# Three products moved between engines and one copy split: a linear-attention and MLP-mixer kernel

## The chip, the cores and the metric

The kernel runs on one core of a Trainium2 chip. The metric is the device time of one execution in microseconds (us), as the median of several runs. A core has five engines with a queue each: TensorE (PE) multiplies matrices and transposes, VectorE (DVE), ScalarE (ACT) and GpSimd (POOL) work element by element, SyncE (SP) issues loads and stores. An engine works off its queue in the order of the program and waits where an operand of the next instruction isn't there yet. TensorE writes its results to PSUM; VectorE and ScalarE read them there; GpSimd works on SBUF.

## The reference

```python
# token mixing: r, k, v of shape (4, 8, 768, 48), per batch and head
state = 0
for t in range(768):
    cur = (u * k[t]) outer v[t]
    y[t] = r[t] @ (state + cur)
    state = w * state + k[t] outer v[t]
# x: (4, 768, 384), heads side by side; then an MLP mixer
h  = relu(x^T @ w_tok1) @ w_tok2         # over the tokens, 768 -> 256 -> 768
u_ = x + h^T
h2 = relu(u_ @ w_ch1) @ w_ch2            # over the channels, 384 -> 1536 -> 384
out = u_ + h2
```

## The kernel before

The 768 tokens of a batch are cut into 6 chunks of 128; the 4 batches give 24 units, numbered 0 to 23, six to a batch. Units 0 to 5 are batch 0 and make the start of the kernel. The steps of a unit, by the names of the code:

- kp and rp: the products of k and of r with a decay table (wn, wp), on GpSimd or VectorE, written to the two halves of a tile kpr. The tables are made on ScalarE from the logarithm of w.
- trk and trr: four transposes each on TensorE, of the k half and of the r half. Both write to one tile tr_ps, which lies in one PSUM bank.
- rkk and rkr: two copies of tr_ps into SBUF (tile rk) on ScalarE. For the units in `rk_two` (0, 1, 2, 3, 4, 6) they are two steps, and each can stand in the queue where its own transposes are done. For the others one step rk issues both copies behind trr.
- at: eight matmuls that give the scores of the 8 heads, in two PSUM tiles (even and odd heads). AT0 and AT1: the two halves multiplied by a triangular mask and written to SBUF in bf16, on VectorE. For the units in `raw` (0, 1, 5, 8, 11) the second half goes another way: raw copies it from PSUM to SBUF on ScalarE, and ATr on VectorE multiplies that copy by a bf16 mask.
- pr, pg, yd: the term of the current token (product, small matmul, product with v).
- kv and S: the state, accumulated in PSUM, and its masked copy; every third copy uses a decay table wGm, a product that is made once, behind gd on ScalarE.
- yS and y: matmuls of r with the state and of the scores with v, into one PSUM tile. x adds yd and writes the unit's output as bf16, on VectorE.
- hid and what follows are the mixer: hid multiplies each x by the first token weight and accumulates over the six units of the batch.

The order on each engine is written by a planner (class `Plan`, function `graph`): it simulates the steps with assumed durations, ranks and due times, and gives each step an engine and a start; the steps are then emitted in the order of their starts. Into gaps of TensorE's plan it puts idle matmuls (`fill`). So the order on an engine is fixed when the program is built, and a step that waits holds up all that stands behind it on its engine.

`products_in_turn` adds waits: a product on GpSimd that stands near a product on VectorE is put behind a VectorE instruction, so that the two don't run side by side. Here rp2 is put behind pr0 and rp3 behind AT1 of unit 1, because kp2 and wGm are planned on VectorE.

In queue order, as far as it is touched: GpSimd has kp0, rp0, kp1, rp1, rp2, kp3, rp3, kp4, the issue of the first token weight, rp4, the issue of the second, kp5, rp5, and the issues of five channel weights. ScalarE has rkk3, rkr3, S3, rkk4, vb4 (a cast of v), rkr4, S4, rk5 (two copies), vb5, raw5. TensorE has at4, trk5, pg4, trr5, yS4, a fill, y4, at5. SyncE issues the loads of units 0 to 5 at once; those of unit 6 and on are held until y5.

All instructions go through one helper, so the profile gives nearly all of them one line; they are told apart by tile and shape (kpr<-ld_k is kp, kpr<-ld_r is rp, rk<-tr_ps the copies, at_ps<-rk the scores, AT the masked halves).

Of the kernel before, what the change touches and what calls it, by code (L numbers as in the profile page):

```python
# [45 lines left out]
class Plan:  # L46
# [83 lines left out]
    def fill(self, since, until, least, margin, each, emit):  # L130

        mine = sorted((s for s in self.steps if s.engine == "PE"), key=lambda s: s.start)
        for a, b in zip(mine, mine[1:]):
            if b.start > until:
                break
            if a.end < since:
                continue
            taken = sum(1 for x in self.used if x[0] < b.start and x[1] > a.end)
            n = int((b.start - a.end - margin) / each)
            if b.start - a.end >= least and taken < self.banks and n > 0:  # L140
                s = self.add(f"fill{a.name}", [("PE", n * each, n * each)], emit=emit(n))
                s.engine, s.start, s.end, s.seen = "PE", a.end, a.end + n * each, a.end + n * each
        return sorted(self.steps, key=lambda s: s.start)


def products_in_turn(steps, apart):


    both = [s for s in steps if s.engine in ("DVE", "POOL") and s.name.rstrip("0123456789") in ("kp", "rp", "ku", "rku", "yd", "wGm")]
    dve = [s for s in steps if s.engine == "DVE"]  # L150
    behind, d = {}, None
    for s in both:
        if s.engine == "DVE":
            d = s if len(s.after) and s.name[:2] != "yd" or s.ways[0][0] == "POOL" else d
        elif d is not None and s.start - d.end < apart:
            n = dve.index(d)
            behind[s] = dve[n - 1] if n and d.start - dve[n - 1].end < 0.05 else d
            d = None
    return behind
# [9 lines left out]
def graph(do, cfg):  # L169
# [246 lines left out]
CFG = dict(apart=2.0,   # L416
    transfers=[("u", u) for u in range(0, 6)]
    + [('k', 6)]
    + [('r', 6)]
    + [('k', 7)]  # L420
    + [('r', 7)]
    + [('v', 6)]
    + [('v', 7)]
    + [('u', 8)]
# [20 lines left out]
    xload={6: 0.33},  # L445
    wtime=(3.0, 2.6, 1.55, 5.2, 3.1, 3.9, 1.55),
    raw=(0, 1, 5, 8, 11),
    rk_two=(0, 1, 2, 3, 4, 6),
    mix=(0.0, 0.0, -1.0, -2.6),
    off3=[{}, {}, {'AT0': -0.12, 'rp': 0.83, 'rku': 1.35}],  # L450
# [17 lines left out]
def kernel(  # L468
# [121 lines left out]
    for i in range(NB):  # L590
        t = const.tile([128, 2, H, P], bf16, name=f"kpr{i}")
# [24 lines left out]
    wGm = const.tile([128, HP, 2, D], f32, name="wGm")  # L616
# [387 lines left out]
    def do(kind, *args):  # L1004
        return lambda eng: STEPS[kind](eng, *args)

    def fill(eng, n):
        t = psM.tile([128, 512], f32, name="fill_ps", tag="m")
        for lo in range(0, n, 2):
            cols = slice(0, 256 * min(2, n - lo))  # L1010
            pe.matmul(t[:, cols], idle[:, 0:128], idle[:, cols], start=True, stop=True)

    plan = graph(do, CFG)
    steps = plan.run()
    if CFG.get("fill"):
        first = next(s for s in steps if s.name == "z0_0_0").start
        steps = plan.fill(CFG.get("fill_from", 0.0), first, *CFG["fill"], lambda n: lambda eng: fill(eng, n))
    behind = products_in_turn(steps, CFG["apart"])
    last = {}
    for s in steps:  # L1020
# [38 lines left out]
```

## Time and profile before

| | |
|---|---|
| median of 3 runs | 165.36 us (164.93 to 165.66) |
| profiled execution | 165.7 us, of it span 164.0 us |
| TensorE busy | 156.6 us |
| VectorE busy | 109.2 us |
| ScalarE busy | 88.5 us |
| GpSimd busy | 67.1 us |

The span runs from the first to the last instruction of the profiled execution; the other 1.7 us of its time lie around it. A row of the timeline gives the start in us, the duration, the engine, the operation with its output and inputs, the number of instructions that are merged in it and, in brackets, how long the engine sat idle before it and what ended that. A row of the chain of waits gives start, duration and the work that the end of the kernel was waiting for at that time.

### The profile page before, as it was taken

Reading aid. Unit: us, or ns where it says so; the run is one execution under the profiler, and the core shown is the slowest. Engines: PE = TensorE matmul, PEld = TensorE weight load, DVE = VectorE, ACT = ScalarE, POOL = GpSimd, SP = SyncE. Lnnn points to the kernel's source line nnn. Section 1 sums busy time; section 2 is a strip of 40 time slices with the busy share of each in tenths; the row PEclk is TensorE's granted clock in tenths of the full one; section 3 lists DMA queues with packets and bytes.
Section 4 is the critical chain, followed back from the end, with each engine's and each line's share of the span. In section 5 each row is a group of like instructions: output and inputs, shape, how many; then the busy total and the mean of one; then the engine's idle time right before and its main releaser. Section 6 shows DMA issues by size and latency. Waiting matters only on the chain.

```text
span 164.0 us, 3852 instructions
## 1 busy us (share of the span) xinstructions
PE 156.6 (95%) x1466; PEld 100.9 (62%) x1466; DVE 109.2 (67%) x225; ACT 88.5 (54%) x194; POOL 67.1 (41%) x83
## 2 busy tenths in 40 slices
PE   6798999999999999899999999999999999999992
PEld 3277865566677666566566565666656655666562
DVE  6679897602289889899899899977876582012021
ACT  3898662595488466789706450077253502914900
POOL 8748893000037848566875856204750000000000
DMA  4999999999798997999999972999990028012012
GB/s 92 221 223 207 173 154 173 192 194 232 153 231 233 190 213 220 196 238 180 217 231 133 263 135 67 203 231 194 194 240 4 0 53 216 19 52 96 0 48 96
DMA packets 87307, 26.26 MB, mean 160 GB/s; under 512 B 76665, under 2 KB 87290, under 8 KB 87290
## 3 DMA queue, kind: packets, MB, share of 16 engines
q1 hardware_dynamic: 83392, 22.88, 65.1%
q0 software_dynamic: 3888, 3.15, 13.1%
q8 instruction: 11, 0.18, 0.4%
q14 instruction: 6, 0.05, 0.2%
q10 hardware_dynamic: 10, 0.00, 0.0%
HBM read 20.65 MB, written 4.72 MB: 155 GB/s over the span
## 4 chain that ended last, share of the span: by engine, by line
PE 85%; DVE 5%; ACT 5%; issue 2%; POOL 1%; DVEq 0%; ACTq 0%
PE h_ps L515 33%; PE z_ps L515 29%; PE y_ps L515 5%; PE at_ps L515 5%; PE tr_ps L515 4%; PE hT_ps L515 3%; PE kv_ps L515 3%; ACT rk L515 2%; DVE AT L515 2%; DVE x_b L515 1%; PE w_ps L515 1%; DVE yd L515 1%; POOL kpr L515 1%; ACT wp L515 1%; ACT raw L515 1%
## 5 line engine op out<-in xcount | busy, mean ns | idle before, releaser
L515 ACT ACTIVATE zr<-z_ps 128x384 bf16<-128x384 f32 x94 | 45.4, 492 | 44.2 <-PE z_ps L515 44.1
L515 PE MATMUL z_ps<-uT,wch 128*128 128x384 bf16 x288 | 52.5, 326 | 0.2
L515 PE MATMUL h_ps<-wch,zr 128*128 128x384 bf16 (+1 forms) x300 | 52.5, 320 | 0.0
L515 PEld LDWEIGHTS <-zr 128*128 128x128 bf16 x300 | 27.9, 98 | 15.5 <-issue 0.2
L515 PEld LDWEIGHTS <-wch 128*128 128x128 bf16 x288 | 26.7, 98 | 16.1 <-issue 0.4
L515 POOL TENSOR_TENSOR yd<-vb,adg 128x384 f32<-128x384 bf16 x18 | 15.5, 859 | 42.2 <-ACT adg L515 25.1
L515 DVE TENSOR_TENSOR AT<-at_ps,mask 128x512 bf16<-128x512 f32 x43 | 27.9, 683 | 0.6 <-PE at_ps L515 0.5
L515 DVE TENSOR_TENSOR osb<-u_sb,h_ps 128x384 f32<-128x384 bf16 (+1 forms) x22 | 11.7, 532 | 23.5 <-PE h_ps L515 23.4
L515 POOL TENSOR_TENSOR kpr<-ld_r,wp 128x384 bf16<-128x384 f32 x16 | 17.0, 1064 | 5.3 <-DVE yd L515 2.2
L515 ACT COPY rk<-tr_ps 128x512 bf16<-128x512 bf16 x28 | 15.5, 589 | 5.5 <-PE tr_ps L515 5.1
L515 PEld LDWEIGHTS <-kpr 128*128 128x128 bf16 x192 | 13.6, 108 | 6.1 <-POOL kpr L515 2.6
L515 DVE TENSOR_TENSOR x_b<-y_ps,yd 128x384 bf16<-128x384 f32 x24 | 13.3, 552 | 5.8 <-PE y_ps L515 5.5
L515 POOL TENSOR_TENSOR kpr<-ld_k,wn 128x384 bf16<-128x384 f32 x15 | 15.5, 1031 | 2.1 <-PE z_ps L515 1.1
L515 PEld LDWEIGHTS <-rk 48*128 48x128 bf16 (+1 forms) x272 | 11.1, 100 | 6.4 <-issue 2.8
L515 PE MATMUL tr_ps<-ident,kpr 128*128 128x128 bf16 x112 | 12.3, 247 | 2.0 <-ACT rk L515 1.0
L515 ACT CAST vb<-ld_v 128x384 bf16<-128x384 f32 x24 | 12.3, 511 | 3.5 <-DMA ld_v<-in_v_dram 3.5
L515 DVE TENSOR_TENSOR u_sb<-x_b,hT_ps 128x384 bf16<-128x384 bf16 x21 | 10.4, 546 | 1.1 <-PE hT_ps L515 1.1
L515 PEld LDWEIGHTS <-wtok 128*128 128x128 bf16 x90 | 8.0, 98 | 4.8 <-issue 0.6
L515 PEld LDWEIGHTS <-AT 128*128 128x128 bf16 x192 | 8.6, 99 | 3.6 <-DVE AT L515 0.7
L515 PE MATMUL at_ps<-rk 48*128 48x128 bf16 x192 | 10.4, 233 | 0.4 <-ACT rk L515 0.4
L515 DVE TENSOR_TENSOR kpr<-ld_k,wn 128x384 bf16<-128x384 f32 x9 | 5.9, 658 | 7.0 <-DMA ld_k<-in_k_dram 7.0
L515 PE MATMUL h_ps<-x_b,wtok 128*128 128x384 bf16 x48 | 10.2, 326 | 0.1
(91 smaller groups left out, 154.2 us busy)
## 6 DMA issues: line engine op xcount, KB each, us to landing
ld_k<-in_k_dram SPq DMA_DIRECT2D x24, 192.0 KB, 3.6
ld_v<-in_v_dram SPq DMA_DIRECT2D x24, 192.0 KB, 3.7
out_dram<-osb SPq DMA_DIRECT2D x23, 192.0 KB, 2.5
ld_r<-in_r_dram SPq DMA_DIRECT2D x28, 96.0 KB, 3.2
ld_r<-in_r_dram SPq DMA_DIRECT2D x10, 192.0 KB, 3.8
wch<-in_moe_w_ch_dram POOLq DMA_DIRECT2D x3, 576.0 KB, 12.6
wtok<-in_moe_w_tok_dram POOLq DMA_DIRECT2D x2, 384.0 KB, 5.1
wch<-in_moe_w_ch_dram POOLq DMA_DIRECT2D x2, 288.0 KB, 5.6
```

What stands on the lines that cost most here:

```text
L515: ins = tc.keep_in_program_order(f(*args, **kw))
```

## The change

A new function `placed` edits the finished plan, behind the planner and the fills, so that no other step changes its place.

- kp2 goes from VectorE to GpSimd at the same place in the order (behind rp1). wGm goes from VectorE to GpSimd, just ahead of rp2. With no such product on VectorE, `products_in_turn` no longer puts rp2 and rp3 behind a VectorE instruction.
- For units 2, 3 and 4, a step raw is put on ScalarE behind the unit's at, and the second half of the scores is masked from that copy (ATr) at its old place on VectorE. On ScalarE raw2 stands between rkk3 and rkr3, raw3 between vb4 and rkr4, raw4 behind S4.
- For unit 5, the copy of the k half is a step rkk5 of its own, put on ScalarE behind trk5 (and behind raw4). In the order of the program it now stands ahead of trr5. The old step copies only the r half.

```diff
+def placed(steps, do, moved, raw, apart):
+    named = {s.name: s for s in steps}
+    for u in raw:
+        s = Step(f"raw{u}", [], (), None, (), 0.0, do("raw", u))
+        s.engine, s.start = "ACT", named[f"at{u}"].end + 0.001
+        s.end = s.seen = s.start + 0.6
+        named[f"AT1_{u}"].emit = do("ATr", u)
+        steps.append(s)
+    for u in apart:
+        s = Step(f"rkk{u}", [], (), None, (), 0.0, do("rkk", u))
+        s.engine, s.start = "ACT", named[f"trk{u}"].end + 0.001
+        s.end = s.seen = s.start + 0.5
+        named[f"rk{u}"].emit = do("rkr", u)
+        steps.append(s)
+    for name, engine, other in moved:
+        s, t = named[name], named[other]
+        s.engine = engine
+        if s is not t:
+            s.start = s.end = s.seen = t.start - 1e-6
+    return sorted(steps, key=lambda s: s.start)
...
     raw=(0, 1, 5, 8, 11),
+    raw_too=(2, 3, 4),
+    rk_apart=(5,),
+    moved=(('kp2', 'POOL', 'kp2'), ('wGm', 'POOL', 'rp2')),
...
+    steps = placed(steps, do, CFG["moved"], CFG["raw_too"], CFG["rk_apart"])
     behind = products_in_turn(steps, CFG["apart"])
```

## The prediction

> **What bounds the kernel now.** I read the page first, for the engine that is full.
>
> ```profile
> span 164.0 us, 3852 instructions
> PE 156.6 (95%) x1466; PEld 100.9 (62%) x1466; DVE 109.2 (67%) x225; ACT 88.5 (54%) x194; POOL 67.1 (41%) x83
> ```
>
> TensorE is busy for 156.6 of 164.0 us. The waits of TensorE from 30 us to the end come next:
>
> ```profile
> PE at_ps L515 <- ACT rk L515: 0.4, 1, 0.4
> PE kv_ps L515 <- ACT vb L515: 0.2, 1, 0.2
> ```
>
> Behind 30 us it waits for 0.6 us in all. So whatever the start gains or loses reaches the end nearly whole, and nothing behind it makes up for it. The change lies ahead of 27 us, so I followed the chain of waits there (start, us, what).
>
> ```profile
> 12.78 0.59 ACT raw L515
> ...
> 16.42 0.20 PE g_ps L515 x4
> ...
> 18.89 0.33 PE y_ps L515 x8
> ...
> 19.24 0.56 DVE x_b L515
> ...
> 26.55 0.57 DVE x_b L515
> ...
> 27.16 0.48 PE h_ps L515 x2
> ```
>
> There are three stretches. Up to 13.9 us ScalarE's queue sets the pace, from 13.9 to 19.24 TensorE, from 19.24 to 27.16 VectorE, until x of unit 5 lets the last token-mixing matmuls of batch 0 start at 27.16. The time of that start is what I work out; a shift of it is a shift of the end. The timeline of TensorE shows the joints:
>
> ```profile
> 13.91 0.59 PE L515 MATMUL tr_ps<-ident,kpr 128*128 128x128 bf16 x4 [0.67 <-ACT rk L515]
> ...
> 17.83 0.63 PE L515 MATMUL tr_ps<-ident,kpr 128*128 128x128 bf16 x4
> ...
> 18.25 0.63 PE L515 MATMUL fill_ps<-idle 128*128 128x512 bf16 x1
> ...
> 19.79 0.38 PE L515 MATMUL tr_ps<-ident,kpr 128*128 128x128 bf16 x4
> ...
> 20.89 0.58 PE L515 MATMUL y_ps<-vb,AT 128*128 128x48 bf16 x8
> 21.41 0.40 PE L515 MATMUL at_ps<-rk 48*128 48x128 bf16 x8
> 21.73 0.40 PE L515 MATMUL tr_ps<-ident,kpr 128*128 128x128 bf16 x4
> ...
> 22.14 0.40 PE L515 MATMUL tr_ps<-ident,kpr 128*128 128x128 bf16 x4
> 22.38 0.33 PE L515 MATMUL y_ps<-S,rk 128*128 128x96 bf16 x4
> 22.55 0.81 PE L515 MATMUL fill_ps<-idle 128*128 128x512 bf16 x3
> 23.20 0.19 PE L515 MATMUL y_ps<-vb,AT 128*128 128x48 bf16 x1
> 23.58 0.35 PE L515 MATMUL y_ps<-vb,AT 128*128 128x48 bf16 x7 [0.20 <-DVE AT L515]
> 23.86 0.40 PE L515 MATMUL at_ps<-rk 48*128 48x128 bf16 x8
> ...
> 25.94 0.45 PE L515 MATMUL y_ps<-vb,AT 128*128 128x48 bf16 x8
> 26.23 0.33 PE L515 MATMUL at_ps<-ident,x_b 128*128 128x128 bf16 x3
> ```
>
> By the order of the code: 13.91 is trr2 (transposes of r, unit 2); 17.83 trk4; 19.79 trr4; 20.89 y3; 21.41 at4 (scores of unit 4); 21.73 trk5 and 22.14 trr5; 22.38 yS4; 22.55 the idle fill; 23.20 and 23.58 y4; 23.86 at5; 25.94 y5.
>
> **Parts 1 and 2: k product of unit 2 and decay table to GpSimd.** The rows of both engines:
>
> ```profile
> 10.64 0.55 DVE L515 TENSOR_TENSOR kpr<-ld_k,wn 128x384 bf16<-128x384 f32 x1
> ...
> 14.69 0.55 DVE L515 TENSOR_TENSOR wGm<-bm,wG 128x384 f32<-128x384 f32 x1
> ```
>
> ```profile
> 12.31 1.13 POOL L515 TENSOR_TENSOR kpr<-ld_r,wp 128x384 bf16<-128x384 f32 x1 [2.24 <-DVE yd L515]
> ...
> 14.85 1.25 POOL L515 TENSOR_TENSOR kpr<-ld_r,wp 128x384 bf16<-128x384 f32 x1 [0.46 <-DVE AT L515]
> ...
> 17.00 0.89 POOL L515 DMA_DIRECT2D wtok<-in_moe_w_tok_dram  x1
> 18.37 0.99 POOL L515 TENSOR_TENSOR kpr<-ld_r,wp 128x384 bf16<-128x384 f32 x1 [0.48 <-DMA ld_r<-in_r_dram]
> ...
> 21.08 1.01 POOL L515 TENSOR_TENSOR kpr<-ld_r,wp 128x384 bf16<-128x384 f32 x1
> ```
>
> GpSimd sits idle from 10.07 to 12.31 (2.24). Two products of 0.99 (the row alone) to 1.25 (the row beside the table on VectorE) take 2.0 to 2.5 us there, so rp2 is 0 to 0.3 late, and ends at 13.44 to 13.74. trr2 starts at 13.91 behind a ScalarE copy, so either end is hidden; I take 0.1. Without that cover it would be the 0.3. VectorE is 2 x 0.55 us lighter, and that is worth nothing either: before 13.9 ScalarE's fixed order sets the pace, after it TensorE does.
>
> In the Trainium skill, "GPSIMD Engine Reference", section "Engine selection", sends two-input elementwise work to VectorE, GpSimd being about twice as slow, and the rows here agree on that ratio (0.55 against 0.99). By that rule taken as a cost on the path the two moves would lose 2 x 0.44 us; by the rows they lose nothing, being under the idle time.
>
> One thing does move. rp3 (14.85) is kept in turn behind a VectorE product only because the table stood on VectorE; that wait goes. kp3 ends at 14.39 (14.85 less 0.46), so rp3 starts up to 0.46 earlier and takes 0.99 for 1.25. kp4 and the issue of the first token-mixing weight (17.00) then come up to 0.7 us earlier, among loads of r, k and v that still run: a rival below.
>
> **Part 3: half the scores of units 2, 3, 4 through ScalarE.** The rows that price it, VectorE first:
>
> ```profile
> 19.78 1.29 DVE L515 TENSOR_TENSOR AT<-at_ps,mask 128x512 bf16<-128x512 f32 x2
> ...
> 24.97 0.68 DVE L515 TENSOR_TENSOR AT<-at_ps,mask 128x512 bf16<-128x512 f32 x1
> 25.57 0.42 DVE L515 TENSOR_TENSOR AT<-raw,mask_b 128x512 bf16<-128x512 bf16 x1
> 25.90 0.55 DVE L515 TENSOR_TENSOR yd<-vb,g_ps 128x384 f32<-128x384 bf16 x1
> ```
>
> ```profile
> 13.27 0.59 ACT L515 COPY rk<-tr_ps 128x512 bf16<-128x512 bf16 x1
> ...
> 22.58 1.07 ACT L515 COPY rk<-tr_ps 128x512 bf16<-128x512 bf16 x2 [1.23 <-PE tr_ps L515]
> ...
> 24.33 0.59 ACT L515 CAST raw<-at_ps 128x512 bf16<-128x512 f32 x1 [0.26 <-PE at_ps L515]
> ```
>
> From start to next start VectorE spends 0.60 on a half read from PSUM (24.97 to 25.57) and 0.33 on one read from SBUF: 0.27 saved each, for a 0.59 us copy on ScalarE. Unit 2 lies in TensorE's stretch: nothing. Unit 3: y3 starts at 20.89 behind the fill as before, but no longer waits inside for the second half. Unhindered y5 passes in 0.29 (25.94 to 26.23, the next matmuls' start), so at4 starts at 21.18 instead of 21.41. Unit 4: VectorE ends its halves about 0.54 earlier, so y4's wait (23.20 to 23.58) would be gone. Left alone, this part gains between 0.2 (only at4's shift) and 0.5 us (below).
>
> **Part 4: k of unit 5 copied apart.** This is where I expect the gain to go. The two halves of one tr tile lie in one PSUM bank, and in the new order the copy of the k half stands between trk5 and trr5. Unit 2 has that order already: its k copy on ScalarE runs 13.27 to 13.86, its r product was ready at 13.44, and trr2 starts at 13.91 with "0.67 <-ACT rk". So transposes into the second half wait for the copy of the first. In the old order trr5 (22.14) followed rp5 (ends 22.09) at once.
>
> In the Trainium skill, "PSUM — Partial Sum Buffer", section "PSUM bank collisions raise a hardware error", says that two engines must not touch one bank and quadrant at once, and that software has to order them; unit 2's wait agrees, 0.05 us behind the copy's end. By that rule trr5 waits always; by the one row alone it might not, which is the second rival.
>
> The sum: at4 21.18, ends 21.58 (0.40). raw4 0.07 later (raw5 came 0.07 behind at5's end, 24.26 to 24.33): 21.65. The copy of k5 stands behind it in ScalarE's queue, 0.49 later (12.78 to 13.27): 22.14, ends 22.73. trr5 22.78, which is 0.64 later than now. TensorE issues in order, so yS4, the fill and y4 stand behind it: 0.24 + 0.17 + 0.65 (22.14 to 22.38, 22.55, 23.20) gives y4 23.84, its halves long ready. at5 0.29 later: 24.13, against 23.86. Its r copy: trr5 ends 23.18, copied to 23.81, in time. From at5 to y5 TensorE has 2.08 us of work and no idle time (23.86 to 25.94): y5 26.21, ends 26.66, x5 about 26.70 against 26.55. The start at 27.16 becomes 27.31: **+0.15 us**. So the wait inside y4 is taken away and a longer one at trr5 takes its place.
>
> Bounds of this part: if at4 does not come earlier, everything is 0.23 later, +0.38; if trr5 is not held, -0.5.
>
> The profiled execution took 165.7 us by itself, so it becomes 165.85. The median of the runs is 165.36, 0.34 lower, with runs from 164.93 to 165.66; against the median I forecast **165.5 us**. About 0.5%, 0.8 us, is what a measurement of this kernel can tell from no change.
>
> **Rivals.** *trr5 is not held* (164.9). Then trr5 stays at 22.14, y4 runs whole at 23.20, at5 starts at 23.49, 0.37 earlier; y5 25.57 to 26.02; x5 at 26.06, 0.49 earlier than now. Against it: the 0.67 at trr2.
>
> *The early weight issue delays r of unit 4* (165.8). rp4 waits for its load until 18.37 (0.48). If the weight's 0.7 us earlier start costs that load 0.65, rp4 ends at 20.01 instead of 19.36, and trr4 (19.79) starts at 20.05: +0.26 on top of 0.15. It decides once the load is over 0.4 late. For it: the load is the last thing that GpSimd waits for. Against: the loads were issued long before.
>
> *TensorE's pace changes earlier* (164.4). Four transposes take 0.63 at 17.83 and 0.38 at 19.79; start to next start it is 0.42 (17.83 to 18.25) against 0.24 (22.14 to 22.38), so TensorE works at some 0.57 of its later pace until then. Had it changed 3 us earlier, the 2.8 us from 16.42 to 19.24 would shrink by up to 1.2; I take 1.1, as unit 2's lighter half on VectorE would then count. *It changes later* (166.4), the rival on the slower side: place 19.8 to 23.2, price 0.43 of 3.4 us, 1.5, less the 0.6 us of waits there (0.23 at y3, 0.38 at y4), so +0.9 on top of 0.15; it decides if the transposes of unit 4 still take 0.6. Against both: the order of TensorE's work before 19.24 is not touched.
>
> In the Trainium skill, "TensorE: Matmul & The Clock Gate", section "Part 1: The HAM clock gate (the "warmup" mystery)", has a free-running window of about 3.4 us behind that change, so that it can fall differently from run to run; the change of pace between 18.25 and 19.79 agrees with a clock released late, and no run here shows the window.
>
> **How the numbers follow.** Forecast 0.55; trr5 not held 0.12; r of unit 4 late 0.13; earlier pace 0.12; later pace 0.08. Faster by over 0.5% (under 164.5) takes the earlier pace, a third of the second case and some of the spread of the runs: 0.20. Slower (over 166.2) takes the later pace and part of the late load: 0.15. The rest, 0.65, is no change. The range, 164.4 to 166.3, reaches from the earlier pace to most of the late load; the forecast's own is 164.9 to 165.9.
>
> **What would show it.** Right: the transposes of unit 5 apart by about 1.2 us, the second with a wait for ScalarE's rk; y4 in one piece; at5 near 24.1; units 3 and 4 with one AT of 0.68 and one of 0.42; TensorE's rows from 13.91 to 19.24 in place. Wrong: trr5 at 22.1 and at5 near 23.5; rp4 behind 18.8; tr_ps rows at 0.38 before 19 or 0.6 after 20.

## The result, and the profile after

The kernel after takes 166.77 us (median; 166.50 to 166.84), the kernel before 165.47 us in the same series (164.93 to 165.66). The ratio is 1.0074, with a 95% interval of 1.0054 to 1.0095: slower by 1.3 us. The profiled execution took 166.83 us.

The page of the kernel after, its head:

```profile
span 165.1 us, 3850 instructions
PE 156.5 (95%) x1466; PEld 100.3 (61%) x1466; DVE 109.9 (67%) x223; ACT 89.9 (54%) x197; POOL 68.5 (41%) x85
```

TensorE has the same work (156.5 against 156.6 us), the span is 1.1 us longer. VectorE gave two products of 0.55 us away and yet is busy for 0.7 us longer. That is the oddity to explain. What TensorE waits for from 30 us to the end (us in total, times, longest):

```profile
PE at_ps L540 <- ACT rk L540: 0.4, 1, 0.4
PE kv_ps L540 <- ACT vb L540: 0.2, 1, 0.2
```

These are the 0.6 us of before, so the 1.1 us arise ahead of 30 us. The chain of waits of the kernel after in that part (start, us, what):

```profile
10.15 0.95 DVE UW L540
...
12.62 0.64 DVE AT L540
...
15.49 1.21 DVE AT L540
16.75 0.46 PE y_ps L540 x7
17.21 0.54 PE at_ps L540 x8
...
23.33 0.50 ACT rk L540
23.87 0.38 PE tr_ps L540 x4
...
28.78 0.33 PE fill_ps L540 x2
```

and the same place of the kernel before:

```profile
27.16 0.48 PE h_ps L515 x2
27.64 0.33 PE fill_ps L515 x2
```

The idle fill starts when the last hid of batch 0 is done: 27.64 before, 28.78 after, 1.14 us later, which is the difference of the spans. Ahead of 15.49 ScalarE no longer sets the pace: the chain runs through VectorE, by instructions that took 0.42 us before (AT) and are now 1.21 long. VectorE's timeline after:

```profile
9.63 1.47 DVE L540 TENSOR_TENSOR UW<-wu_sb 64x4 bf16<-64x4 f32 x2
11.13 0.42 DVE L540 TENSOR_TENSOR pr<-tr_ps,rk 128x512 bf16<-128x512 bf16 x1
...
12.53 1.10 DVE L540 TENSOR_TENSOR AT<-raw,mask_b 128x512 bf16<-128x512 bf16 x1
...
15.42 1.28 DVE L540 TENSOR_TENSOR AT<-raw,mask_b 128x512 bf16<-128x512 bf16 x1
...
18.48 0.41 DVE L540 TENSOR_TENSOR AT<-raw,mask_b 128x512 bf16<-128x512 bf16 x1
...
21.41 0.54 DVE L540 TENSOR_TENSOR AT<-raw,mask_b 128x512 bf16<-128x512 bf16 x1
...
23.73 0.41 DVE L540 TENSOR_TENSOR AT<-raw,mask_b 128x512 bf16<-128x512 bf16 x1
```

and GpSimd's:

```profile
10.09 0.99 POOL L540 TENSOR_TENSOR kpr<-ld_k,wn 128x384 bf16<-128x384 f32 x1
11.04 0.82 POOL L540 TENSOR_TENSOR wGm<-bm,wG 128x384 f32<-128x384 f32 x1
12.36 1.00 POOL L540 TENSOR_TENSOR kpr<-ld_r,wp 128x384 bf16<-128x384 f32 x1 [0.50 <-ACT wp L540]
...
14.46 1.00 POOL L540 TENSOR_TENSOR kpr<-ld_r,wp 128x384 bf16<-128x384 f32 x1
15.41 1.00 POOL L540 TENSOR_TENSOR kpr<-ld_k,wn 128x384 bf16<-128x384 f32 x1
16.35 0.89 POOL L540 DMA_DIRECT2D wtok<-in_moe_w_tok_dram  x1
```

Read side by side: UW, one pair of products of 64x4, ends at 11.10, when kp2 (10.09 + 0.99 = 11.08) ends. The masked half of unit 0 comes at 12.53, 0.17 behind the start of rp2, and lasts until 13.63; rp2 ends at 13.36. The half of unit 1 comes at 15.42, 0.01 behind the start of kp4, and lasts until 16.70; kp4 ends at 16.41. Between them pr reads one operand from PSUM (tr_ps) and takes its usual 0.42 beside wGm. So a VectorE instruction that takes both operands from SBUF seems to stand still while a GpSimd product runs that was first. Against before it is held 0.78 us at UW (1.47 for 0.69), 0.68 (1.10 for 0.42) and 0.87 (1.28 for 0.41), and 0.13 at the half of unit 3 beside rp5 (20.67 to 21.66): 2.46 us in all. Each held half ends 0.27 to 0.29 us behind the end of the product's row (13.63 and 13.36, 16.70 and 16.41, 21.95 and 21.66), whatever its own start was. Ahead of y1 (the scores of unit 1 with v) stand the first three holds, 2.33 us, and of the products that left VectorE only kp2 (0.46 from start to next start): the half of unit 1 ends 1.93 us later than before (16.70 against 14.77), of which 0.05 is there at UW already. The scores of unit 2 (at2) start at 17.14 instead of 15.81, 1.33 later.

The trace of before shows the same thing small. The group of the tile UW in the kernel before (min/median/max in ns), and GpSimd's row beside it:

```profile
L515 DVE TENSOR_TENSOR UW<-wu_sb x2: 163/336/508, 9.6 to 10.1; 64x4 bf16<-64x4 f32 x2
```

```profile
9.08 0.99 POOL L515 TENSOR_TENSOR kpr<-ld_r,wp 128x384 bf16<-128x384 f32 x1
```

Two equal instructions, one of 163 ns and one of 508. The long one starts at 9.58 and ends at 10.09; rp1 ends at 10.07. It is held by rp1 for 0.35 us. In the kernel after kp2 stands right behind rp1 and holds the second one too: the pair takes 509 and 946 ns there.

In the Trainium skill, "SBUF — State Buffer", section "Who interferes with whom", says that a VectorE instruction with two SBUF inputs contends with a GpSimd instruction that reads SBUF, that the ports which the two engines share are an exclusive lock and the order of issue decides who blocks, and that a VectorE instruction with at most one SBUF input, outside the modes that use two ports, does not contend. The rows above agree (0.68 and 0.87 us of hold with two SBUF inputs, none for pr beside wGm), and the prediction had not used it.

### The profile page after: what moved, and what is told of

It is laid out like the page before. It is cut to its first block, busy times and chain, and to the rows that moved or that the text cites. A ratio compares the mean times of both kernels' runs of the same rounds, so it can differ in the third digit from the quotient of the medians.

```text
span 165.1 us, 3850 instructions
## 1 busy us (share of the span) xinstructions
PE 156.5 (95%) x1466; PEld 100.3 (61%) x1466; DVE 109.9 (67%) x223; ACT 89.9 (54%) x197; POOL 68.5 (41%) x85
## 4 chain that ended last, share of the span: by engine, by line
PE 86%; DVE 6%; ACT 3%; issue 2%; POOL 1%; DVEq 0%; ACTq 0%
PE h_ps L540 34%; PE z_ps L540 29%; PE y_ps L540 5%; PE at_ps L540 5%; PE tr_ps L540 4%; PE hT_ps L540 3%; PE kv_ps L540 3%; DVE AT L540 2%; ACT rk L540 1%; PE w_ps L540 1%; PE fill_ps L540 1%; DVE UW L540 1%; POOL kpr L540 1%; DVE yd L540 1%; ACT vb L540 1%
## 5 line engine op out<-in xcount | busy, mean ns | idle before, releaser
L540 POOL TENSOR_TENSOR yd<-vb,adg 128x384 f32<-128x384 bf16 x18 | 15.4, 855 | 43.8 <-ACT adg L540 26.3
L540 DVE TENSOR_TENSOR AT<-at_ps,mask 128x512 bf16<-128x512 f32 x40 | 26.1, 682 | 0.6 <-PE at_ps L540 0.5
L540 POOL TENSOR_TENSOR kpr<-ld_k,wn 128x384 bf16<-128x384 f32 x16 | 16.6, 1038 | 2.9 <-PE z_ps L540 1.1
L540 PE MATMUL y_ps<-vb,AT 128*128 128x48 bf16 x192 | 9.5, 186 | 0.8 <-DVE AT L540 0.8
```

Source lines behind the costliest of these rows:

```text
L540: ins = tc.keep_in_program_order(f(*args, **kw))
```

## The experiments

Theory A: it is this hold; the start of the loss is kp2 behind rp1. Rivals: B, the loss lies in parts 3 and 4 (trr5, or ScalarE's longer queue); C, the table wGm or the r products, now out of turn, come late on GpSimd. All ratios are against the kernel before on the same chip (165.55 to 165.66 us). Each diff shows the settings in which a run differs from the kernel after or from the run ahead of it; parts of the change that a run leaves out are named in the text. `turns` is a list of pairs: the first step waits for the second.

**The moves alone** (parts 1 and 2), and **the copies alone** (parts 3 and 4):

```diff
-    raw_too=(2, 3, 4),
-    rk_apart=(5,),
+    raw_too=(),
+    rk_apart=(),
```

> Parts 1 and 2 alone: k product of unit 2 and decay table on GpSimd, nothing else changed. Theory A (a VectorE instruction with two SBUF operands is held while GpSimd works on SBUF, as the UW pair of 1.47 for 0.69 us and the masked halves of 1.10 and 1.28 for 0.42 us suggest): 1.0 to 1.4 us slower than before, with UW near 1.5 and the two masked halves of units 0 and 1 near 1.1 and 1.3. Theory B (the loss is the wait of trr5 behind the copy of k5, larger than forecast): within 0.3 us of before. Theory C (the extra copies of the scores hold up ScalarE's queue): within 0.3 us of before.

```diff
-    moved=(('kp2', 'POOL', 'kp2'), ('wGm', 'POOL', 'rp2')),
+    moved=(),
```

> Parts 3 and 4 alone: scores of units 2 to 4 through ScalarE, k of unit 5 copied apart; k product of unit 2 and decay table stay on VectorE. Theory A: +0.15 us against before, as the prediction's own sum for these parts (-0.1 to +0.4), with trr5 held by ScalarE's rk for 0.6 us or more. Theory B: 1.0 us or more slower. Theory C: 0.8 us or more slower.

The moves alone: 166.61 us, ratio 1.0051 (1.0028 to 1.0073). In VectorE's and GpSimd's timeline of this run:

```profile
9.53 1.47 DVE L540 TENSOR_TENSOR UW<-wu_sb 64x4 bf16<-64x4 f32 x2
...
12.43 1.10 DVE L540 TENSOR_TENSOR AT<-raw,mask_b 128x512 bf16<-128x512 bf16 x1
...
15.31 0.42 DVE L540 TENSOR_TENSOR AT<-raw,mask_b 128x512 bf16<-128x512 bf16 x1
```

```profile
15.31 1.27 POOL L540 TENSOR_TENSOR kpr<-ld_k,wn 128x384 bf16<-128x384 f32 x1
```

UW and the half of unit 0 are held as in the kernel after. At 15.31 VectorE came first by less than the 0.01 us that the rows resolve: there VectorE keeps its 0.42 and GpSimd's product takes 1.27 for 0.99. Who is held is decided by who is first, and being second costs VectorE 0.87 but GpSimd 0.27. This profiled execution took 165.55 us, 1.06 less than the median and no more than the kernel before, so its rows show where the holds arise and not what the median lost. In the slower executions (six of ten lie at 166.58 to 166.74) the half of unit 1 may have come second and been held too; no profile shows it. By the median the moves alone lose 1.05 us, so B isn't needed for most of the loss.

The copies alone should have cost 0.15, and took 166.90 us, ratio 1.011 (1.0073 to 1.0148). This miss is the same hold in another place. VectorE, GpSimd and TensorE of this run:

```profile
19.90 1.98 DVE L540 TENSOR_TENSOR AT<-raw,mask_b 128x512 bf16<-128x512 bf16 x1
```

```profile
19.63 1.01 POOL L540 TENSOR_TENSOR kpr<-ld_k,wn 128x384 bf16<-128x384 f32 x1
20.59 1.00 POOL L540 TENSOR_TENSOR kpr<-ld_r,wp 128x384 bf16<-128x384 f32 x1
```

```profile
21.93 0.35 PE L540 MATMUL y_ps<-vb,AT 128*128 128x48 bf16 x7 [1.44 <-DVE AT L540]
```

The half of unit 3, which part 3 has made an instruction with two SBUF operands, comes 0.27 behind kp5, and is held past kp5 and past rp5 as well: one product behind the other passed it by. TensorE waits 1.44 us for it. In the kernel after the shift by parts 1 and 2 happens to move that half to 21.41, where it is held for 0.13 only. So part 3 has this risk in it too.

**Which move, and does an order mend it?** kp2 alone moved, and the same with kp2 told to wait for UW:

```diff
-    moved=(('kp2', 'POOL', 'kp2'), ('wGm', 'POOL', 'rp2')),
+    moved=(('kp2', 'POOL', 'kp2'),),
```

> Only the k product of unit 2 goes to GpSimd; the decay table stays on VectorE, so rp3 keeps its turn behind the masked half of unit 1. Theory A: UW near 1.5 and the masked half of unit 0 near 1.1, but that of unit 1 at 0.42; 0.4 to 0.8 us slower than before. If the product is simply slower on GpSimd (0.99 for 0.55 us) and nothing is held: within 0.2 us, since trk2 has 0.3 us of slack.

```diff
+    turns=(('kp2', 'uw'),),
...
     behind = products_in_turn(steps, CFG["apart"])
+    named = {s.name: s for s in steps}
+    behind.update({named[a]: named[b] for a, b in CFG["turns"]})
```

> As the run with the k product of unit 2 alone on GpSimd, but that product waits for the end of UW on VectorE. Theory A: UW back at 0.69, the masked half of unit 0 back at 0.42, time within 0.2 us of before, although GpSimd does the same work and starts it 0.2 us later. If the loss came from GpSimd's slowness or from its load: as slow as without the wait, or slower.

kp2 alone: 166.16 us, ratio 1.0063 (1.0039 to 1.0087), UW 1.47 and the half of unit 0 1.10. In turn: 165.13 us, 0.9985 (0.9968 to 1.0002); UW 0.69 at 9.53, kp2 at 10.35, the half of unit 0 0.42 at 11.68.

```profile
9.53 0.69 DVE L541 TENSOR_TENSOR UW<-wu_sb 64x4 bf16<-64x4 f32 x2
```

```profile
10.35 1.00 POOL L541 TENSOR_TENSOR kpr<-ld_k,wn 128x384 bf16<-128x384 f32 x1 [0.33 <-DVE UW L541]
```

A start of kp2 that is 0.3 us later makes the kernel 1.0 us faster. That it lies 0.4 under the kernel before by the median, where within 0.2 was expected, isn't shown to be a gain: the interval includes 1. kp2 alone is 0.6 us slower than the kernel before by the medians and 1.0 by the ratio, so the hold behind kp2 is the cause of the larger part of the loss.

The table alone on GpSimd (kp2 back on VectorE, no copies):

```diff
+    moved=(('wGm', 'POOL', 'rp2'),),
```

> Part 2 alone: the decay table on GpSimd, the k product of unit 2 on VectorE; rp3 has lost its turn. Theory A: UW at 0.69; the table lies between rp1 and rp2 where VectorE has one-SBUF-operand work or the k product of unit 2; the masked half of unit 1 starts near 14.4, as rp3 does, and is held for up to 1 us if it comes second. Between no change and 0.6 us slower, decided by that row.

165.07 us, 0.9983 (0.9966 to 1.0000). The halves of units 0 and 1 come ahead of rp2 and beside rp3 (12.12 and 14.32) and take 0.42 each; rp2 and rp3 take 1.14 and 1.27. C falls: the table costs nothing by itself, and the r products out of turn don't either while VectorE is first.

**Is it the operands in SBUF?** The moves alone, with the halves of units 0 and 1 masked straight from PSUM (no raw0, raw1):

```diff
+    for u in (0, 1):
+        named[f"AT1_{u}"].emit = do("AT", u, 1)
+        steps.remove(named[f"raw{u}"])
```

> Parts 1 and 2 as in the run that has them alone, but the second halves of units 0 and 1 are masked from PSUM on VectorE, without ScalarE's copy, so that these instructions have one operand in SBUF. Theory A (two operands in SBUF are what is held): UW still near 1.5, but both halves at 0.68 beside GpSimd's products; 0.2 to 0.8 us faster than that run although VectorE's own work grows by 0.5 us. If any VectorE instruction is held beside GpSimd: halves at 1.1 to 1.3, no faster.

165.54 us, 1.0008 (0.9992 to 1.0024), 1.07 us less than with the moves alone. VectorE and GpSimd of this run:

```profile
12.43 0.69 DVE L543 TENSOR_TENSOR AT<-at_ps,mask 128x512 bf16<-128x512 f32 x1
...
15.25 0.68 DVE L543 TENSOR_TENSOR AT<-at_ps,mask 128x512 bf16<-128x512 f32 x1
```

```profile
12.22 0.99 POOL L543 TENSOR_TENSOR kpr<-ld_r,wp 128x384 bf16<-128x384 f32 x1 [0.46 <-ACT wp L543]
...
15.08 1.00 POOL L543 TENSOR_TENSOR kpr<-ld_k,wn 128x384 bf16<-128x384 f32 x1
```

Both halves come 0.2 behind the start of a GpSimd product and neither is held, where the half of unit 0 was held for 0.68 from the same 0.2 with the moves alone. UW, which has two SBUF operands still, takes 1.47 here too. GpSimd has the same products in the same order here, so their order or number alone doesn't hold a VectorE instruction; an operand in SBUF in place of PSUM does. The 1.07 us of the kernel need not be the holds alone, as two copies of 0.59 us have left ScalarE's queue too; it is the durations of the halves that tell.

**The split of the copy alone** (part 4):

```diff
-    raw_too=(2, 3, 4),
-    moved=(('kp2', 'POOL', 'kp2'), ('wGm', 'POOL', 'rp2')),
+    raw_too=(),
+    moved=(),
```

> Part 4 alone: k of unit 5 copied apart, all else as before. By the prediction's sum: copy of k5 22.15 to 22.74, trr5 22.79 instead of 22.14, at5 at 24.14 instead of 23.86, +0.1 to +0.3 us. If trr5 is not held: at5 0.3 us earlier or equal, 0 to -0.2 us.

165.64 us, 0.9993 (0.9976 to 1.0011). The transposes stand as summed, with the second set released by ScalarE's copy:

```profile
21.23 0.40 PE L540 MATMUL tr_ps<-ident,kpr 128*128 128x128 bf16 x4
...
22.30 0.38 PE L540 MATMUL tr_ps<-ident,kpr 128*128 128x128 bf16 x4 [0.60 <-ACT rk L540]
```

From at4 to at5 TensorE takes 2.73 us against 2.45 before, the 0.28 of the sum. But behind at5 x of unit 5 comes in 2.48 instead of 2.69, so 0.07 of it is left, and the time shows nothing.

**Putting the change in order.** All parts but the table's move, with kp2 behind UW and kp5 behind the half of unit 3, and the same without the split copy; then kp2 behind UW with two copied halves (units 2 and 4), without the split and without the turn of kp5:

```diff
-    moved=(('kp2', 'POOL', 'kp2'), ('wGm', 'POOL', 'rp2')),
+    moved=(('kp2', 'POOL', 'kp2'),),
+    turns=(('kp2', 'uw'), ('kp5', 'AT1_3')),
```

> The change with its overlaps taken away: k product of unit 2 on GpSimd behind UW, decay table left on VectorE (so rp3 keeps its turn), k product of unit 5 behind the masked half of unit 3; scores of units 2 to 4 through ScalarE and k of unit 5 copied apart, as in the change. Theory A (two-SBUF-operand instructions of VectorE held for the length of GpSimd's products are the whole loss of the change): every half masked from SBUF at 0.42, UW 0.69, trr5 still held by ScalarE's rk; time within 0.3 us of before, the prediction's +0.15 included. If the split copy of k5 or the copies on ScalarE lose something large: 0.8 us or more slower.

```diff
-    rk_apart=(5,),
+    rk_apart=(),
```

> As the run with the overlaps taken away, but the copies of unit 5 stand together behind trr5, as before the change. If trr5 waits for the copy of k5 only by the order: trr5 follows rp5 at once (rp5 now about 0.2 us later than before), at5 0.1 to 0.3 us earlier than with the split, 0.1 to 0.3 us faster than it. If the split gains: slower than it.

```diff
-    raw_too=(2, 3, 4),
+    raw_too=(2, 4),
+    turns=(('kp2', 'uw'),),
```

> A version that takes what the runs so far leave of the change: k product of unit 2 on GpSimd behind UW, and the second halves of units 2 and 4 alone through ScalarE (GpSimd issues weights in those places and multiplies nothing); unit 3, the decay table and unit 5 as before the change. Theory A: no instruction held; 0.2 to 0.6 us faster than before. If copies on ScalarE cost more than they save: no gain over the run with the k product alone in turn.

All three missed: 166.57 us (1.0055, 1.0034 to 1.0077), 166.76 (1.0068, 1.0045 to 1.0090) and 165.71 (1.0003, 0.9983 to 1.0022). In each the half of unit 2, now at 17.06 to 17.23, took 1.94 or 1.95 us. The rows of the third:

```profile
17.06 1.94 DVE L541 TENSOR_TENSOR AT<-raw,mask_b 128x512 bf16<-128x512 bf16 x1
```

```profile
16.78 0.90 POOL L541 DMA_DIRECT2D wtok<-in_moe_w_tok_dram  x1
17.70 1.01 POOL L541 TENSOR_TENSOR kpr<-ld_r,wp 128x384 bf16<-128x384 f32 x1
```

It comes while GpSimd issues a weight, 0.64 us ahead of rp4's row, and ends 0.29 behind rp4's end (18.71). Either the issue holds it or the product queued behind it does. The second of the three misses was to be 0.1 to 0.3 us faster than the first and came out 0.2 slower, which their spreads don't tell apart: without the split trr5 waits for rp5, which the turn of kp5 makes late (23.63 against 23.72 with the split), and at5 stands behind both copies (25.19 against 25.05). To tell issue from product, rp4 was put behind the half of unit 2:

```diff
+    turns=(('kp2', 'uw'), ('rp4', 'AT1_2')),
```

> As the run with two halves (units 2 and 4) through ScalarE, where the half of unit 2 masked from SBUF took 1.94 us, but the r product of unit 4 on GpSimd waits for that half; the issue of the first weight stays ahead of it. If the half was held by the r product alone: 0.42 us. If the issue of the weight holds it too: it ends with the issue, 0.9 to 1.1 us. If neither holds it (the operand copied by ScalarE came late): still 1.9. Time 0.2 to 0.6 us under the run with two halves in the first two cases.

165.24 us, 0.9975 (0.9958 to 0.9992).

```profile
17.15 0.42 DVE L541 TENSOR_TENSOR AT<-raw,mask_b 128x512 bf16<-128x512 bf16 x1
```

```profile
16.86 0.89 POOL L541 DMA_DIRECT2D wtok<-in_moe_w_tok_dram  x1
17.77 1.01 POOL L541 TENSOR_TENSOR kpr<-ld_r,wp 128x384 bf16<-128x384 f32 x1
```

The half lies wholly inside the issue and isn't held; only rp4's wait is new. So the issue doesn't hold it, the queued product does, and that from before its own row begins. It isn't so for any start inside the issue: in the run with the copies alone, without a turn, the same half came 0.07 behind the start of the issue (0.28 in the run with two halves), with rp4's row at 17.88, and wasn't held.

```profile
17.04 0.42 DVE L540 TENSOR_TENSOR AT<-raw,mask_b 128x512 bf16<-128x512 bf16 x1
```

```profile
16.97 0.89 POOL L540 DMA_DIRECT2D wtok<-in_moe_w_tok_dram  x1
```

So by these two profiles being first is decided between 0.84 and 0.64 us ahead of the product's row. Whether the product lays hold of its operands that early, or its row starts late in the profile, is open.

With a copy for unit 4 only, which meets no product, nothing needs a new turn beside kp2's:

```diff
+    raw_too=(4,),
+    turns=(('kp2', 'uw'),),
```

> k product of unit 2 on GpSimd behind UW, and only the second half of unit 4 through ScalarE, where GpSimd issues weights and multiplies nothing. Theory A: that half at 0.42, no instruction held; 0.2 to 0.7 us faster than before, 0.3 us or more faster than the run with two halves. If masking from SBUF costs in itself: not faster than the run with the k product alone in turn.

165.18 us, 0.9979 (0.9963 to 0.9994): the half takes 0.41 at 22.97.

Last, the change with every conflict ordered away: kp2 on GpSimd behind UW (the table stays on VectorE), or the table on GpSimd and kp2 on VectorE; and the table with two halves.

```diff
+    moved=(('kp2', 'POOL', 'kp2'),),
+    turns=(('kp2', 'uw'), ('rp4', 'AT1_2'), ('kp5', 'AT1_3')),
```

> All four parts of the change but the decay table's move (which alone lost nothing), with each product of GpSimd that overlapped put behind the VectorE instruction it held: k of unit 2 behind UW, r of unit 4 behind the half of unit 2, k of unit 5 behind the half of unit 3. Theory A: no masked half over 0.45 us, trr5 held by ScalarE's rk as forecast; within -0.3 to +0.4 us of before, the prediction's +0.15 among them, and 0.7 us or more faster than the changed kernel. If more than the overlaps and part 4 is in the loss: 0.8 us or more slower than before.

```diff
+    moved=(('wGm', 'POOL', 'rp2'),),
+    turns=(('rp4', 'AT1_2'), ('kp5', 'AT1_3')),
```

> The changed kernel with its decay table on GpSimd, its three copied halves and its split copy of unit 5, but the k product of unit 2 back on VectorE, and two turns (r of unit 4 behind the half of unit 2, k of unit 5 behind the half of unit 3). Theory A: UW at 0.69, halves of units 0 to 3 at 0.42; within 0.4 us of before either way.

```diff
+    moved=(('wGm', 'POOL', 'rp2'),),
+    raw_too=(2, 4),
+    rk_apart=(),
+    turns=(('rp4', 'AT1_2'),),
```

> The best of the parts together: decay table on GpSimd, k product of unit 2 on VectorE, second halves of units 2 and 4 through ScalarE with r of unit 4 in turn behind the first of them, unit 5 as before the change. Theory A: 0.3 to 0.8 us faster than before. If the gains of the table's move and of the halves are the same VectorE time: 0.2 to 0.4 us, as each alone.

The first: 165.68 us, 1.0026 (1.0010 to 1.0042). UW 0.69, the halves of units 0 to 3 0.42 or 0.43, that of unit 4 0.70 beside rp5. Of the 1.3 us 0.1 (by the medians) to 0.4 (by the ratio) are left, and the turn of kp5 has a price of its own: TensorE waits for it.

```profile
21.58 0.40 PE L541 MATMUL tr_ps<-ident,kpr 128*128 128x128 bf16 x4 [0.55 <-POOL kpr L541]
```

The second: 166.10 us, 1.0050 (1.0029 to 1.0070), 0.4 more than the first, and a miss: by the medians 0.5 over the kernel before, where within 0.4 was expected. No half is held there beyond those of the first (unit 4: 0.71), and its profile agrees with the first's but for a shift of 0.15 us that is there at 9.5 us already. What makes its median 0.4 longer isn't settled. The third: 165.30 us, 0.9992 (0.9974 to 1.0010); the 0.3 to 0.8 us that it should have gained don't show. trr5 stands at 22.09 there, released by rp5 ("0.86 <-POOL kpr"), where it was before (22.14): in its profile what the halves save ahead of trr5 goes into that wait.

By the ratio the fastest kernels are the one with rp4 behind the half of unit 2 and the one with unit 4 alone, 0.2% under the kernel before, with intervals that end at 0.9992 and 0.9994. kp2 in turn (165.13 us, 0.9985) and the table alone (165.07 us, 0.9983) lie inside the same intervals, so no run shows that a copied half adds anything to the moves.

## Why the prediction was wrong

**What bounds the kernel: right.** The end of the last hid moved by 1.14 us and the span by 1.1; behind 30 us TensorE waits for the same 0.6.

**Parts 1 and 2, "worth nothing": this step failed.** The prediction put two sentences in it: the cover of GpSimd's idle 2.24 us, and "VectorE is 2 x 0.55 us lighter, and that is worth nothing either". Both products fit under the idle time as summed (0.99 and 0.82; rp2 at 12.36 against 12.31), and that is not where the price lies. The sum priced an overlap of the two engines by GpSimd's side, 0.99 to 1.25, and left VectorE's side at nothing. That price is right only where VectorE is first. Nor did ScalarE and TensorE keep setting the pace: the chain of the kernel after runs through VectorE up to 16.70 us. Where GpSimd is first, VectorE's instruction with two SBUF operands waits: 0.78, 0.68 and 0.87 us here, 1.3 us later at2, 1.1 at x2. The profile of before had the row, 508 ns beside 163 ns for two equal instructions of UW, and the kernel's own `products_in_turn`, which exists to keep such pairs apart, was read as something that only costs a wait.

**The r product of unit 3 out of its turn: seen, and its danger put in the wrong place.** The prediction had rp3, kp4 and the first weight up to 0.7 us earlier; they are 0.4 to 0.65 earlier (14.46, 15.41, 16.35). It looked for the harm at the load of unit 4's r. There was none: rp4 runs at 17.27 right behind the weight. The harm was that kp4 now meets the masked half of unit 1 at 15.4 (0.87 us).

**TensorE's rows from 13.91 to 19.24 "in place": wrong** for that reason, 14.38 for trr2 and 17.14 for at2.

**Parts 3 and 4: right at trr5 and y4; the gain at y3 didn't come.** x2 is 1.10 later (20.34 against 19.24). The rows of TensorE after:

```profile
21.78 0.57 PE L540 MATMUL y_ps<-vb,AT 128*128 128x48 bf16 x8
22.28 0.40 PE L540 MATMUL at_ps<-rk 48*128 48x128 bf16 x8
22.61 0.40 PE L540 MATMUL tr_ps<-ident,kpr 128*128 128x128 bf16 x4
...
23.87 0.38 PE L540 MATMUL tr_ps<-ident,kpr 128*128 128x128 bf16 x4 [0.78 <-ACT rk L540]
...
25.21 0.40 PE L540 MATMUL at_ps<-rk 48*128 48x128 bf16 x8
```

at4 comes 0.87 later than before, so 0.23 less than x2, which is the size of the summed gain (0.23) and yet luck. From y3's start to at4's it takes 0.50 (21.78 to 22.28) against 0.52 before: the wait inside y3 is still there, as the half of unit 3 is held and ends at 21.95. The other 0.21 comes from TensorE's change of pace, which fell earlier in its order of work: from at3 to the next matmuls it takes 0.33 after (20.23 to 20.56) and 0.54 before (19.14 to 19.68).

From at4 on the sum fits. Against at4, trr5 is 0.86 later than before (summed: 0.87), released by ScalarE's copy of k5, and at5 0.48 later (summed: 0.50), with y4 in one piece. Of this 0.48, 0.21 is regained behind at5, as in the split alone: y5 takes 0.36 us for the 0.45 that the sum kept, and x5 no longer stands behind yd in VectorE's queue. So "a longer one at trr5 takes its place" holds.

The whole shift of the last hid in the two profiles is then 1.33 at at2, less 0.44 by the change of pace up to y3, less 0.02 inside y3, plus 0.48 up to at5, less 0.21 behind it: 1.14 us. Parts 3 and 4 have 0.25 of it, where 0.15 was summed. That they cost no more is partly luck too: without the shift by parts 1 and 2 the half of unit 3 meets kp5 and is held 1.56 us.

**The rivals.** "trr5 is not held" and "r of unit 4 late" didn't happen. TensorE's change of pace fell at about 19.7 us in the profiles of both kernels (y2 starts at 18.68 before and 19.94 after, at3 0.46 behind it before and 0.29 after). As the holds had moved TensorE's work to later times, it gave back 0.44 of at2's 1.33 (y3 comes 0.89 later). None of the rivals on the slower side was the hold, so 166.77 lies 0.47 outside the range, and "slower" had a chance of 0.15.

## What to carry to other kernels

Before work is moved from VectorE to GpSimd, list VectorE's instructions that take both operands from SBUF, and look at which GpSimd products will be running or queued when each comes: if GpSimd is first, add what is left of its products to VectorE's path. Turning an operand in PSUM into a copy in SBUF makes an instruction shorter when alone (0.42 for 0.68 us) and puts it into that list. Two equal instructions of unlike duration in one group's minimum and maximum can be the sign of a hold that is there already, and a wait that looks useless (a product in turn) may be what keeps it small.

## What was not expected of the hardware

- A held VectorE instruction can be passed by two GpSimd products in a row (1.98 us for 0.42, past kp5 and rp5), and by one whose row starts 0.64 us after its own (1.94 us).
- The hold is lopsided: VectorE second loses up to 1.56 us, GpSimd second 0.14 to 0.28 (1.13 to 1.27 us for 0.99).
- The issue of a weight from GpSimd's queue (0.89 us) doesn't hold such an instruction (0.42 us inside it).
- TensorE's change of pace, at about 19.7 us in the profiles of the kernels before and after, came anywhere from about 17.2 us (table with two halves) to 20.5 (unit 4 alone) in the others, and the page's granted clock doesn't show it. It came at about 17.6 with kp2 in turn (profiled run 164.71 us, 0.4 below its median) and at about 18.6 with the moves alone (165.55, 1.1 below its median). So one profile and the median of the runs can lie 1 us apart. With the moves alone the close order of the half of unit 1 and kp4 is a second reason, and the runs don't tell the two apart. The runs of the kernel before, some near 164.9 and most near 165.6, may be the change of pace; no profile of that kernel is of a run near 164.9.
